# Decay sums one unit earlier, zeroing spread over eight units, the first expert's weights two units later

## The chip, the cores and the metric

The kernel runs on one core of a Trainium2 chip. The metric is device time in microseconds (us) of one execution, as the median of several runs. TensorE is PE in the rows, VectorE is DVE, ScalarE is ACT, GpSimd is POOL, and SyncE, which issues most transfers, is SP.

## The reference

Three layers follow each other. The first is a gated linear attention over 4 sequences of 768 steps with 8 heads of 48; the second sends each of the 3072 rows to one of 8 experts; the third is a gated layer over all rows.

```python
f = 1.0 / (1.0 + np.exp(-f_logit))
for t in range(S):
    state = f[:, :, t, :, None] * state + np.einsum('bhd,bhe->bhde', k[:, :, t], v[:, :, t])
    y[:, :, t] = np.einsum('bhd,bhde->bhe', q[:, :, t], state)
...
e_idx = np.argmax(x @ w_gate, axis=1)
for e in range(E):
    mask = e_idx == e
    h = np.maximum(x[mask] @ w1[e], 0.0)
    out[mask] = gate_w[mask, None] * eom[mask, e, None] * (h @ w2[e])
...
return (1.0 / (1.0 + np.exp(-(x @ w_gate))) * (x @ w_val)) @ w_out
```

## The kernel before, in words

The attention is cut into 24 units of 128 steps, 6 to a sequence. A loop over i = 1 to 23 writes the instructions of several units into each round, and each engine carries its own out in the order written. For a unit u the steps are these. `s_log` and `s_log2` (ACT) make the logarithm of the decays from the tile `ft`. `s_sum` (DVE) sums them along the steps with a scan, 1.2 us long. `s_keys` takes an exponential of the sums on ACT (`gi`) and multiplies the keys by it on DVE (`kT`); `s_queries` takes the other exponential on ACT, in place, and multiplies the queries on POOL (`qT`). `s_end` (ACT) keeps the last decay of each head (`gc_all`). `s_turn` transposes `kT` (PE) and copies it (ACT). `s_score` multiplies keys and queries (PE, `pS`), and `s_mask` masks the result in two halves (DVE, `am`). `s_state` (PE, DVE) carries the state on, `s_y` makes the outputs (PE, `pY`) and copies them (ACT, `xT`), and `s_rows` turns them back into rows together with the router's logits (PE `px`, ACT `x`, DVE `lg`).

Round i holds, in this order: score(i), keys and queries(i+1), the masks of i, y(i-1), state(i), turn(i+1), rows(i-1); log and sum stand in it for unit i+2. So the sum that keys(i+1) reads in round i was written by DVE near the end of round i-1.

Three more kinds of work are woven in. The inputs are asked for ahead on SP's queue (`load`): keys and queries of unit i+4, decays of i+6, values of i+4. A table in HBM, `xs_all`, that later holds each expert's rows, has the rear of each expert's part filled with zeros by 8 transfers from `zrow`, and takes the rows themselves by indirect transfers from POOL (`put_rows`) once `route` has given a group of units their places (on DVE, in short steps that `step_route` takes one or two of per round; the groups are units 0-5, 6-11, 12-16, 17-21, 22-23). And the weights of the first expert come in 10 transfers into 5 staging buffers (`feed.issue`), from which each `feed.step` splits one piece into two parts (ACT `w_hi`, DVE `w_lo`), 14 pieces in all.

After round 23 the expert layer begins with expert 0's first 192 rows (`gather_rows(0)`, `scale`, `to_xt`), whose units call `make_plan` in steps; the plan orders the other experts. `gather_rows(1)`, expert 0's other rows, waits for all rows put.

Of the kernel before, what the change touches and what calls it, by code (L numbers as in the profile page):

```python
# [8 lines left out]
F32 = mybir.dt.float32  # L9
# [3 lines left out]
AF = mybir.ActivationFunctionType  # L13
ALU = mybir.AluOpType
# [6 lines left out]
P = 128  # L21
# [7 lines left out]
def kernel(  # L29
# [17 lines left out]
    nc = tc.nc  # L47
    B, H, S, D = q.shape
    NT, DM = out.shape
    NE = moe_w_gate.shape[1]  # L50
# [3 lines left out]
    HP = H // 2  # L54
# [4 lines left out]
    NB = 4  # L59
    SLOT = NB * P  # L60
# [4 lines left out]
    XW = DM + 2  # L65
# [11 lines left out]
    LEAST = 256  # L77

    PD = P // 2 + D
# [15 lines left out]
    xs_all = drp.tile([NSL, XW], F32, name="xs_all")  # L95
# [391 lines left out]
    st = {}  # L487
# [21 lines left out]
    with ExitStack() as actx:  # L509
# [20 lines left out]
        def load(nm, u):  # L530
            if 0 <= u < NU and (nm, u) not in tin:
                b, c = divmod(u, NCH)
                if nm == "v":
                    t = inp.tile([P, H, D], F32, name="v", bufs=5)
                    nc.sync.dma_start(t.rearrange("p h d -> p (h d)"), v[u * P : (u + 1) * P, :])
                else:
                    t, src = (fts[u % NFT], ft) if nm == "f" else (qks[u % NQK], qkt)
                    for j in (1, 0):
                        nc.sync.dma_start(t[j * (P // 2) : j * (P // 2) + D], src[b, c, j])
                tin[nm, u] = t  # L540

        def s_log(u):

            ln = wk.tile([PD, HP, P], F32, name="ln")
            nc.scalar.activation(out=ln, in_=tin["f", u], func=AF.Exp, scale=-1.0)
            st[u] = dict(ln=ln)

        def s_log2(u):
            ln = st[u]["ln"]
            nc.scalar.activation(out=ln, in_=ln, func=AF.Ln, bias=1.0)  # L550

        def s_sum(u):

            d = st[u]
            d["ls"] = wk.tile([PD, HP, P], F32, name="ls")
            nc.vector.tensor_tensor_scan(  # L556
                out=d["ls"].rearrange("p h t -> p (h t)"), data0=runs01.rearrange("p h t -> p (h t)"),
                data1=d["ln"].rearrange("p h t -> p (h t)"), initial=0.0, op0=ALU.mult, op1=ALU.add,
            )

        def s_keys(u):
# [17 lines left out]
        def s_end(u):  # L579

            nc.scalar.copy(gc_all[:, u, :], st[u]["g"][:, :, P - 1])
# [89 lines left out]
        with tc.manual_schedule():  # L671
            nc.scalar.preload_act_table_set("natural_log_exp_and_others")
            feed.todo = expert_items(0, 0)
            rows_between(nc.vector, fts[0], 30.0)
            nc.gpsimd.memset(oneb, 1.0)
            keep_warm(NWARM)
            nc.vector.memset(rw[D - D % 32 : P // 2, :, PD:], 0.0)
            load("f", 0)
            rows_between(nc.gpsimd, qks[0], 0.0)
            rows_between(nc.vector, fts[1], 30.0)  # L680
            load("f", 1)
            load("qk", 0)
# [12 lines left out]
            load("qk", 2)  # L695
            rows_between(nc.vector, fts[3], 30.0)
            load("f", 3)
            load("v", 1)
            load_router(rw)
            numbers()  # L700
            for u in (0, 1):
                s_log(u)
                s_log2(u)
                load("f", u + 4)
                s_sum(u)
            for u in (0, 1):
                s_keys(u)
                s_queries(u)
                load("v", u + 2)
                load("qk", u + 3)  # L710
            s_turn(0)
            keep_warm(WARM[0])
            s_score(0)
            s_end(0)
            s_log(2)
            s_log2(2)
            s_turn(1)
            load("f", 6)
            load("v", 4)
            for j in range(2):  # L720
                s_mask(0, j)
            s_sum(2)
            s_state(0)
            constants()
            keep_warm(WARM[1])
            groups = [(0, 6), (6, 6), (12, 5), (17, 5), (22, 2)]
            routing = []

            def step_route():
                if routing and next(routing[0], True):  # L730
                    routing.pop(0)

            def on(fn, u, *a):
                if 0 <= u < NU:
                    fn(u, *a)

            for i in range(1, NU):
                if i == NU - 1:
                    gather_rows(0)
                s_score(i)  # L740
                if i == 1:
                    s_log(i + 2)
                    s_log2(i + 2)
                    s_mask(i, 0)
                on(s_keys, i + 1)
                on(s_queries, i + 1)
                load("qk", i + 4)
                on(s_end, i)
                put_rows(2 if i < 19 else 3 if i < 22 else 6)
                if i > 1:  # L750
                    on(s_log, i + 2)
                    s_mask(i, 0)
                load("f", i + 6)
                s_mask(i, 1)
                if i == 1:
                    s_sum(i + 2)
                step_route()
                s_y(i - 1)
                if i > 1:
                    on(s_log2, i + 2)  # L760
                load("v", i + 4)
                s_state(i)
                if i > 1:
                    on(s_sum, i + 2)
                on(s_turn, i + 1)
                if i == 6:
                    feed.issue()
                if i >= 8:
                    feed.step(1)
                if i == LAST:  # L770
                    scale(xg[0], passes[0][2], nc.vector)
                    s_y(i)
                for _ in range(2 if i == LAST else i > 16):
                    step_route()
                s_rows(i - 1)
                for u0, n in groups:
                    if i - 1 == u0 + n - 1:
                        routing.append(route(u0, n))
                if i == 1:
                    nc.gpsimd.memset(zrow, 0.0)  # L780
                if 2 <= i < 6:

                    for e in (2 * i - 4, 2 * i - 3):
                        nc.sync.dma_start(
                            xs_all[e * SLOT + LEAST : (e + 1) * SLOT, :].rearrange("(b p) d -> p b d", p=P),
                            zrow.to_broadcast([P, NB - LEAST // P, XW]),
                        )
            while feed.left():
                feed.step()
            to_xt(0, xg[0], passes[0][2])  # L790
            for todo in routing:
                for _ in todo:
                    pass
            put_rows(6)
            s_rows(LAST)
            for part in range(2):
                put_ids(0, part)
            routing = route(*groups[-1])
            next(routing)

    with ExitStack() as mctx:
# [234 lines left out]
        with tc.manual_schedule():  # L1036
# [24 lines left out]
            for i in range(len(units) + LAG):  # L1061
# [19 lines left out]
                if i < len(units):  # L1081
                    p, f = units[i]
                    if planning:
                        for _ in range(1 if i == 2 else 2):
                            next(planning, None)
                    elif i == 1:
                        for _ in routing:
                            pass
                        put_rows(6)
                        gather_rows(1)  # L1090
                        planning = make_plan()
# [303 lines left out]
```

## Time and profile before

| | |
|---|---|
| median of 3 runs | 847.55 us (847.43 to 851.27) |
| the profiled execution: its time, its span | 854.3 us, 852.5 us |
| PE busy | 823.2 us, 97% |
| DVE, ACT, POOL busy | 450.2, 353.5, 166.9 us |
| moved by all transfers | 87.56 MB |

The span is that of the instructions, the time includes what lies around it. The attention takes about the first 140 us, the expert layer the next 245, the last layer the rest. "Busy" is the sum of instruction times: an engine that is busy 97% over the whole need not be so in each stretch.

### The profile page before, as it was taken

What the parts mean: (1) busy time and instruction counts of PE and PEld (TensorE: products, weight loads), DVE (VectorE), ACT (ScalarE), POOL (GpSimd) and SP (SyncE); (2) the same over time, 40 slices, a digit from 0 to 9 for tenths busy, and PEclk for the clock granted to TensorE, in tenths of its full rate; (3) what the DMA queues carried; (4) which work ended last, traced back from release to release, by engine and by line L of the source; (5) the groups of instructions that cost most, each with busy time, mean ns of one, the idle gap of its engine ahead of it and who ended that gap; (6) DMA issues with size and microseconds to landing.
All of it is one profiled execution on the core that took longest, in us unless ns stands there. A gap on an engine that the chain in (4) does not pass through costs nothing.

```text
span 852.5 us, 13950 instructions
## 1 busy us (share of the span) xinstructions
PE 823.2 (97%) x5289; PEld 727.7 (85%) x5289; DVE 450.2 (53%) x896; ACT 353.5 (41%) x738; POOL 166.9 (20%) x172
## 2 busy tenths in 40 slices
PE   8898989999999999999999999999999999999995
PEld 5776777998899999998888888888888888888884
DVE  6787997568878988997552213222222221232211
ACT  7677874375556665654342212212221221122211
POOL 4225475102323333332000100100010010001001
PEclk9999999999999999999999999999999999999999
DMA  6999762666667767634000200110020010001001
GB/s 158 258 283 266 192 177 82 217 208 196 208 191 224 222 212 218 204 104 139 1 1 1 74 1 1 38 38 0 1 75 1 0 38 2 1 1 38 1 1 40
DMA packets 51645, 87.56 MB, mean 103 GB/s; under 512 B 12874, under 2 KB 32754, under 8 KB 51570
## 3 DMA queue, kind: packets, MB, share of 16 engines
q1 hardware_dynamic: 44946, 62.97, 26.0%
q0 software_dynamic: 6624, 23.62, 8.6%
q8 instruction: 43, 0.70, 0.4%
q14 instruction: 32, 0.26, 0.1%
HBM read 68.35 MB, written 18.22 MB: 102 GB/s over the span
## 4 chain that ended last, share of the span: by engine, by line
issue 51%; PE 32%; DMA 6%; DVE 4%; ACT 3%; POOL 2%; SPq 0%; POOLq 0%; DVEq 0%; ACTq 0%
PE ph L812 5%; PE po L812 5%; PE po L814 5%; PE po L813 5%; PE ph L813 4%; PE ph L814 4%; DMA qk<-in_qkt_dram 4%; POOL out_dram L1022 2%; DMA xs_all<-zrow 1%; DMA ft<-in_ft_dram 1%; PE ptx L430 1%; DVE ls L556 1%; PE pY L653 1%; ACT gi L565 1%; PE px L494 1%
## 5 line engine op out<-in xcount | busy, mean ns | idle before, releaser
L1150 DVE TENSOR_TENSOR hf<-pv,sg 128x512 f32<-128x512 f32 x72 | 49.8, 692 | 266.7 <-PE pv L814 263.1
L1146 ACT ACTIVATE sg<-pg 128x512 f32<-128x512 f32 x72 | 43.1, 598 | 172.8 <-PE pg L814 172.8
L1153 ACT CAST hh<-hf 128x512 fp32r<-128x512 f32 x72 | 44.7, 620 | 161.1 <-DVE hf L1150 152.2
L1022 POOL DMA_INDIRECT out_dram<-ob,ids x24 | 23.6, 983 | 411.4 <-DVE ob L1021 405.9
L813 PE MATMUL po<-w_lo,hh 128*128 128x384 f32 x288 | 96.6, 335 | 0.0
L812 PE MATMUL po<-w_hi,hh 128*128 128x384 f32 x288 | 96.4, 335 | 0.0
L814 PE MATMUL po<-w_hi,hl 128*128 128x384 f32 x288 | 96.3, 334 | 0.0
L814 PE MATMUL pg<-xt_hi,w_lo 128*128 128x512 f32 x216 | 85.5, 396 | 0.0
L813 PE MATMUL pv<-xt_lo,w_hi 128*128 128x512 f32 x216 | 85.5, 396 | 0.0
L812 PE MATMUL pg<-xt_hi,w_hi 128*128 128x512 f32 x216 | 85.5, 396 | 0.0
L813 PE MATMUL pg<-xt_lo,w_hi 128*128 128x512 f32 x216 | 85.1, 394 | 0.0
L812 PE MATMUL pv<-xt_hi,w_hi 128*128 128x512 f32 x216 | 85.1, 394 | 0.0
L814 PE MATMUL pv<-xt_hi,w_lo 128*128 128x512 f32 x216 | 85.1, 394 | 0.0
L244 DVE TENSOR_TENSOR w_lo<-st,w_hi 128x384 fp32r<-128x384 f32 (+1 forms) x112 | 68.9, 647 | 13.9 <-ACT w_hi L243 13.2
L1154 DVE TENSOR_TENSOR hl<-hf,hh 128x512 fp32r<-128x512 f32 x72 | 49.9, 693 | 49.4 <-ACT hh L1153 49.4
L812 PE MATMUL po<-hh,w_hi 128*128 128x192 f32 (+8 forms) x216 | 74.2, 343 | 0.0
L814 PE MATMUL po<-hh,w_lo 128*128 128x192 f32 (+8 forms) x216 | 74.1, 343 | 0.0
L813 PE MATMUL po<-hl,w_hi 128*128 128x192 f32 (+8 forms) x216 | 73.9, 342 | 0.0
L812 PE MATMUL ph<-xt_hi,w_hi 128*128 128x304 f32 (+7 forms) x192 | 67.9, 354 | 0.9 <-DVE hl L1073 0.9
L193 POOL TENSOR_SCALAR cva<-cva 128x512 f32<-128x512 f32 (+1 forms) x30 | 56.3, 1875 | 62.4 <-ACT cva L192 62.1
L1072 ACT ACTIVATE hh<-ph 128x192 fp32r<-128x192 f32 (+8 forms) x72 | 35.6, 494 | 79.1 <-PE ph L814 73.3
L243 ACT CAST w_hi<-st 128x384 fp32r<-128x384 f32 (+1 forms) x112 | 59.3, 558 | 21.9 <-PE po L813 20.0
(173 smaller groups left out, 1658.1 us busy)
## 6 DMA issues: line engine op xcount, KB each, us to landing
st<-in_moe_w_dram SPq DMA_DIRECT2D x48, 256.0 KB
st<-in_moe_w_dram SPq DMA_DIRECT2D x32, 384.0 KB
qk<-in_qkt_dram SPq DMA_DIRECT2D x48, 192.0 KB
ft<-in_ft_dram SPq DMA_DIRECT2D x48, 96.0 KB
v<-in_v_dram SPq DMA_DIRECT2D x24, 192.0 KB
stg<-in_moe_w_gate_dram POOLq DMA_DIRECT2D x9, 512.0 KB
stg<-in_moe_w_val_dram POOLq DMA_DIRECT2D x9, 512.0 KB
stg<-in_moe_w_out_dram POOLq DMA_DIRECT2D x12, 384.0 KB
```

What stands on the lines that cost most here:

```text
L193: nc.gpsimd.tensor_scalar(out=af, in0=af, scalar1=HW_LEAST, scalar2=HW_MOST, op0=ALU.max, op1=ALU.min)
L243: nc.scalar.copy(hi, src)
L244: nc.vector.tensor_tensor(out=lo, in0=src, in1=hi.bitcast(F32), op=ALU.subtract)
L812: nc.tensor.matmul(ps, lhsT=ah, rhs=bh, start=first, stop=False)
L813: nc.tensor.matmul(ps, lhsT=ah, rhs=bl, start=False, stop=False)
L814: nc.tensor.matmul(ps, lhsT=al, rhs=bh, start=False, stop=last)
L1022: put = nc.gpsimd.indirect_dma_start(out=out[:, :], out_offset=bass.IndirectOffsetOnAxis(ap=idx[g][:, i : i + 1], axis=0), in_=ob, in_offs ...
L1072: nc.scalar.activation(out=hh, in_=pS, func=AF.Relu)
L1146: nc.scalar.activation(out=sg, in_=pg, func=AF.Sigmoid)
L1150: nc.vector.tensor_tensor(out=hf, in0=pv, in1=sg, op=ALU.mult)
L1153: nc.scalar.copy(hh, hf)
L1154: nc.vector.tensor_tensor(out=hl, in0=hf, in1=hh.bitcast(F32), op=ALU.subtract)
```

## The change

The logarithm, its sum and the exponential of a unit share one tile `ls` with 4 buffers, and the scan works in place. From round 4 on, log and sum stand in round i for unit i+3; round 4 does two units' logs. The next decays are asked for in `s_log`. `s_end` moves one unit ahead. The zeroing stands in rounds 2 to 9, one expert each. `feed.issue` moves from round 6 to 8 and `feed.step` from 8 on to 10 on. In round 23 the first step of the routing stands ahead of the masks, and the other two behind `s_rows(22)`. In the expert layer each step of the plan is taken one unit later.

```diff
 def s_log(u):
-    ln = wk.tile([PD, HP, P], F32, name="ln")
-    nc.scalar.activation(out=ln, in_=tin["f", u], func=AF.Exp, scale=-1.0)
-    st[u] = dict(ln=ln)
+    ls = wk.tile([PD, HP, P], F32, name="ls", bufs=4)
+    nc.scalar.activation(out=ls, in_=tin["f", u], func=AF.Exp, scale=-1.0)
+    st[u] = dict(ls=ls)
+    load("f", u + NFT)
...
-                on(s_end, i)
+                on(s_end, i + 1)
+                if 1 < i <= LEAD:
+                    s_log(i + 2)
+                    s_log2(i + 2)
                 put_rows(2 if i < 19 else 3 if i < 22 else 6)
-                if i > 1:
-                    on(s_log, i + 2)
-                    s_mask(i, 0)
-                load("f", i + 6)
+                if i >= LEAD:
+                    on(s_log, i + 3)
+                if i == LAST:
+                    step_route()
+                s_mask(i, 0)
                 s_mask(i, 1)
-                if i == 1:
+                if i <= LEAD:
                     s_sum(i + 2)
-                step_route()
+                if i < LAST:
+                    step_route()
                 s_y(i - 1)
-                if i > 1:
-                    on(s_log2, i + 2)
+                if i >= LEAD:
+                    on(s_log2, i + 3)
                 load("v", i + 4)
                 s_state(i)
-                if i > 1:
-                    on(s_sum, i + 2)
+                if i >= LEAD:
+                    on(s_sum, i + 3)
                 on(s_turn, i + 1)
-                if i == 6:
+                if i == 8:
                     feed.issue()
-                if i >= 8:
+                if i >= 10:
                     feed.step(1)
                 if i == LAST:
+                    s_y(i)
                     scale(xg[0], passes[0][2], nc.vector)
-                    s_y(i)
-                for _ in range(2 if i == LAST else i > 16):
+                elif i > 16:
                     step_route()
                 s_rows(i - 1)
+                if i == LAST:
+                    step_route()
+                    step_route()
...
-                if 2 <= i < 6:
-
-                    for e in (2 * i - 4, 2 * i - 3):
-                        nc.sync.dma_start(
-                            xs_all[e * SLOT + LEAST : (e + 1) * SLOT, :].rearrange("(b p) d -> p b d", p=P),
+                if 2 <= i < 2 + NE:
+
+                    nc.sync.dma_start(
+                        xs_all[(i - 2) * SLOT + LEAST : (i - 1) * SLOT, :].rearrange("(b p) d -> p b d", p=P),
...
-                        for _ in range(1 if i == 2 else 2):
+                        for _ in range(min(i - 2, 2)):
                             next(planning, None)
```

The first place is SP's queue at the first weights. Before, this is the end of round 5 and round 6: `qk`, `ft` and `v` are the inputs, `xs_all<-zrow` a zeroing, `st` a load of weights.

```order
L539 DMA qk_114<-in_qkt_dram 48x1024 x2
L539 DMA ft_113<-in_ft_dram 48x512 x2
L535 DMA v<-in_v_dram 128x384
L784 DMA xs_all<-zrow 128x2x386 x2
L539 DMA qk_115<-in_qkt_dram 48x1024 x2
L539 DMA ft_110<-in_ft_dram 48x512 x2
L535 DMA v<-in_v_dram 128x384
L252 DMA st_748<-in_moe_w_dram 128x512
L252 DMA st_750<-in_moe_w_dram 128x512
L252 DMA st_752<-in_moe_w_dram 128x512
L259 DMA st_754<-in_moe_w_dram 128x2x384
L259 DMA st_756<-in_moe_w_dram 128x2x384
```

With the change, this is round 8 and the end of round 9:

```order
L539 DMA qk_114<-in_qkt_dram 48x1024 x2
L539 DMA ft_113<-in_ft_dram 48x512 x2
L535 DMA v<-in_v_dram 128x384
L252 DMA st_914<-in_moe_w_dram 128x512
L252 DMA st_916<-in_moe_w_dram 128x512
L252 DMA st_918<-in_moe_w_dram 128x512
L259 DMA st_920<-in_moe_w_dram 128x2x384
L259 DMA st_922<-in_moe_w_dram 128x2x384
L790 DMA xs_all<-zrow 128x2x386
L539 DMA qk_115<-in_qkt_dram 48x1024 x2
L539 DMA ft_110<-in_ft_dram 48x512 x2
L535 DMA v<-in_v_dram 128x384
```

The five loads of weights stand two rounds later, one zeroing stands behind them, and one more behind the next round's inputs.

The second place is ACT in round 4. Before, one exponential (L545) and one logarithm (L550) stand around the copies of `pY`:

```order
L565 ACTIVATE gi<-ls 112x512
L574 ACTIVATE ls<-ls 112x512
L581 COPY gc_all<-ls 112x4
L545 ACTIVATE ln<-ft_112 112x512
L668 COPY xT<-pY 112x2x128 x2
L550 ACTIVATE ln<-ln 112x512
L500 COPY x<-px 128x2x96
L500 COPY x<-px 128x2x2x48
```

With the change, two more activations stand ahead of those copies:

```order
L564 ACTIVATE gi<-ls 112x512
L573 ACTIVATE ls<-ls 112x512
L580 COPY gc_all<-ls 112x4
L545 ACTIVATE ls<-ft_112 112x512
L551 ACTIVATE ls<-ls 112x512
L545 ACTIVATE ls<-ft_113 112x512
L667 COPY xT<-pY 112x2x128 x2
L551 ACTIVATE ls<-ls 112x512
L500 COPY x<-px 128x2x96
L500 COPY x<-px 128x2x2x48
```

The third place is DVE in round 23. Before, the two masks (`am`) come first, then the first step of the routing (`m` to `oh`), the scaling of the first rows gathered (`xs`), and the ranking, which reads `pr`:

```order
L607 TENSOR_TENSOR am<-pS,tri 128x512 x2
L167 TENSOR_REDUCE m<-lg 128x5
L168 TENSOR_TENSOR t_2248<-lg,m 128x40
L169 TENSOR_TENSOR sc<-lg,m 128x40
L170 TENSOR_TENSOR sc<-sc,e_75 128x40
L171 TENSOR_REDUCE ms_all<-sc 128x5
L172 TENSOR_TENSOR oh<-sc,ms_all 128x40
L441 TENSOR_SCALAR xs<-xs 128x384
L441 TENSOR_SCALAR xs<-xs 64x384
L176 TENSOR_TENSOR ohf<-oh,lg 128x40
L177 TENSOR_REDUCE sel<-ohf 128x5
L347 TENSOR_TENSOR t_2316<-pr,oh 128x40
```

With the change:

```order
L171 TENSOR_REDUCE ms_all<-sc 128x5
L172 TENSOR_TENSOR oh<-sc,ms_all 128x40
L606 TENSOR_TENSOR am<-pS,tri 128x512 x2
L244 TENSOR_TENSOR w_lo<-st_1659,w_hi 128x384
L441 TENSOR_SCALAR xs<-xs 128x384
L441 TENSOR_SCALAR xs<-xs 64x384
L505 TENSOR_REDUCE lg<-px 128x16
L176 TENSOR_TENSOR ohf<-oh,lg 128x40
L177 TENSOR_REDUCE sel<-ohf 128x5
L347 TENSOR_TENSOR t_2301<-pr,oh 128x40
```

The masks stand behind the first step, the last piece of weights (`w_lo`) is in this round, and `lg`, which reads the products `px` of unit 22, stands ahead of the ranking.

## Rows read from the trace of the kernel before

**Rows 1.** Windows, all engines: stretch, busy us, granted clock, DMA share, GB/s.

```profile
40.00:60.00 20.00, 18.77 (x293) 16.13 (x293) 15.75 (x33) 15.51 (x40) 4.15 (x5) 1.00 1.05 299
60.00:80.00 20.00, 17.30 (x228) 14.46 (x228) 15.07 (x35) 14.45 (x37) 10.04 (x12) 0.91 0.99 239
80.00:100.00 20.00, 17.58 (x280) 14.81 (x277) 18.82 (x44) 17.05 (x45) 8.53 (x8) 1.00 0.87 249
160.00:180.00 20.00, 20.00 (x154) 19.77 (x153) 13.26 (x28) 12.93 (x30) 0.00 (x0) 1.00 0.68 218
```

**Rows 2.** Timeline of PE: start, us, line, operation, idle before and its releaser.

```profile
31.91 1.16 PE L600 MATMUL pS<-qT,kT 48*128 48x128 f32 x16
35.21 1.16 PE L494 MATMUL px<-rw,xT 112*128 112x128 f32 x8
...
45.48 1.16 PE L600 MATMUL pS<-qT,kT 48*128 48x128 f32 x16
...
71.18 0.60 PE L588 MATMUL pk<-ident,kT 112*128 112x112 f32 x4 [1.38 <-DVE kT L567]
...
142.54 0.34 PE L812 MATMUL ph<-xt,w_hi 128*128 128x192 f32 x1
```

**Rows 3.** Timeline of DVE, same columns, where it waited.

```profile
52.47 0.69 DVE L567 TENSOR_TENSOR kT<-qk,gi 112x512 f32<-112x512 f32 x1 [0.58 <-ACT gi L565]
...
57.88 0.69 DVE L244 TENSOR_TENSOR w_lo<-st,w_hi 128x512 fp32r<-128x512 f32 x1 [1.19 <-ACT w_hi L243]
...
64.92 0.69 DVE L567 TENSOR_TENSOR kT<-qk,gi 112x512 f32<-112x512 f32 x1 [0.63 <-DMA qk<-in_qkt_dram]
...
72.90 1.27 DVE L556 TENSOR_TENSOR_SCAN ls<-runs,ln 112x512 f32<-112x512 f32 x1 [0.58 <-ACT ln L550]
...
80.25 0.36 DVE L635 TENSOR_TENSOR sn<-pM,gc_all 112x192 f32<-112x192 f32 x1 [3.23 <-PE px L494]
...
106.27 1.23 DVE L556 TENSOR_TENSOR_SCAN ls<-runs,ln 112x512 f32<-112x512 f32 x1 [0.58 <-ACT ln L550]
...
134.88 1.29 DVE L607 TENSOR_TENSOR am<-pS,tri 128x512 f32<-128x512 f32 x2 [0.65 <-PE pS L600]
...
160.56 1.06 DVE L441 TENSOR_SCALAR xs<-xs 128x384 f32<-128x384 f32 x3
```

**Rows 4.** DMA issues by tensor: queue, count, size of one.

```profile
st<-in_moe_w_dram SPq DMA_DIRECT2D x48, 256.0 KB
st<-in_moe_w_dram SPq DMA_DIRECT2D x32, 384.0 KB
qk<-in_qkt_dram SPq DMA_DIRECT2D x48, 192.0 KB
ft<-in_ft_dram SPq DMA_DIRECT2D x48, 96.0 KB
v<-in_v_dram SPq DMA_DIRECT2D x24, 192.0 KB
...
xs_all<-zrow SPq DMA_DIRECT2D x8, 386.0 KB
```

**Rows 5.** Windows, the stretch in which the clock stood at half.

```profile
73.50:76.90 3.40, 3.40 (x36) 2.85 (x32) 3.11 (x6) 2.54 (x7) 2.93 (x4) 0.50 1.07 256
```

**Rows 6.** Timeline of ACT in round 4.

```profile
33.94 0.63 ACT L545 ACTIVATE ln<-ft 112x512 f32<-112x512 f32 x1
34.72 0.65 ACT L668 COPY xT<-pY 112x256 f32<-112x256 f32 x2 [0.15 <-PE pY L662]
```

**Rows 7.** Timeline of POOL: the first put, and the first after round 23.

```profile
72.91 1.16 POOL L385 DMA_INDIRECT xs_all<-x,sidx  x1 [0.18 <-POOL x L383]
...
142.01 1.00 POOL L385 DMA_INDIRECT xs_all<-x,sidx  x1 [0.23 <-POOL xlate L383]
```

**Rows 8.** Timeline of SP's queue: the gathers of the next rows.

```profile
153.82 3.17 SPq L459 DMA_DIRECT2D xs<-xs_all  x3
```

**Rows 9.** Waits from 141 to 172 us: who, for whom, total, times, longest.

```profile
PE pf L904 <- DVE chk L901: 1.6, 1, 1.6
```

More of the change, by code (lines that the diff above doesn't have):

```diff
@@ L542, in s_log @@
         def s_log(u):
-            ln = wk.tile([PD, HP, P], F32, name="ln")
-            nc.scalar.activation(out=ln, in_=tin["f", u], func=AF.Exp, scale=-1.0)
-            st[u] = dict(ln=ln)
+            ls = wk.tile([PD, HP, P], F32, name="ls", bufs=4)
+            nc.scalar.activation(out=ls, in_=tin["f", u], func=AF.Exp, scale=-1.0)
+            st[u] = dict(ls=ls)
+            load("f", u + NFT)
         def s_log2(u):
-            ln = st[u]["ln"]
-            nc.scalar.activation(out=ln, in_=ln, func=AF.Ln, bias=1.0)
+            ls = st[u]["ls"]
+            nc.scalar.activation(out=ls, in_=ls, func=AF.Ln, bias=1.0)
         def s_sum(u):
-            d = st[u]
-            d["ls"] = wk.tile([PD, HP, P], F32, name="ls")
+            ls = st[u]["ls"].rearrange("p h t -> p (h t)")
             nc.vector.tensor_tensor_scan(
-                out=d["ls"].rearrange("p h t -> p (h t)"), data0=runs01.rearrange("p h t -> p (h t)"),
-                data1=d["ln"].rearrange("p h t -> p (h t)"), initial=0.0, op0=ALU.mult, op1=ALU.add,
+                out=ls, data0=runs01.rearrange("p h t -> p (h t)"), data1=ls, initial=0.0, op0=ALU.mult, op1=ALU.add,
             )
@@ L703 @@
                 s_log2(u)
-                load("f", u + 4)
                 s_sum(u)
@@ L714 @@
             s_end(0)
+            s_end(1)
             s_log(2)
@@ L717 @@
             s_turn(1)
-            load("f", 6)
             load("v", 4)
@@ L725 @@
             keep_warm(WARM[1])
+            LEAD = 4
             groups = [(0, 6), (6, 6), (12, 5), (17, 5), (22, 2)]
@@ L747 @@
                 load("qk", i + 4)
-                on(s_end, i)
+                on(s_end, i + 1)
+                if 1 < i <= LEAD:
+                    s_log(i + 2)
+                    s_log2(i + 2)
                 put_rows(2 if i < 19 else 3 if i < 22 else 6)
-                if i > 1:
-                    on(s_log, i + 2)
-                    s_mask(i, 0)
-                load("f", i + 6)
+                if i >= LEAD:
[3 more added lines that the diff above has]
+                s_mask(i, 0)
                 s_mask(i, 1)
-                if i == 1:
+                if i <= LEAD:
                     s_sum(i + 2)
-                step_route()
+                if i < LAST:
+                    step_route()
                 s_y(i - 1)
-                if i > 1:
-                    on(s_log2, i + 2)
+                if i >= LEAD:
+                    on(s_log2, i + 3)
                 load("v", i + 4)
                 s_state(i)
-                if i > 1:
-                    on(s_sum, i + 2)
+                if i >= LEAD:
+                    on(s_sum, i + 3)
                 on(s_turn, i + 1)
-                if i == 6:
+                if i == 8:
                     feed.issue()
-                if i >= 8:
+                if i >= 10:
                     feed.step(1)
                 if i == LAST:
+                    s_y(i)
                     scale(xg[0], passes[0][2], nc.vector)
-                    s_y(i)
-                for _ in range(2 if i == LAST else i > 16):
+                elif i > 16:
                     step_route()
                 s_rows(i - 1)
+                if i == LAST:
+                    step_route()
+                    step_route()
                 for u0, n in groups:
@@ L780 @@
                     nc.gpsimd.memset(zrow, 0.0)
-                if 2 <= i < 6:
-                    for e in (2 * i - 4, 2 * i - 3):
-                        nc.sync.dma_start(
-                            xs_all[e * SLOT + LEAST : (e + 1) * SLOT, :].rearrange("(b p) d -> p b d", p=P),
-                            zrow.to_broadcast([P, NB - LEAST // P, XW]),
-                        )
+                if 2 <= i < 2 + NE:
+                    nc.sync.dma_start(
+                        xs_all[(i - 2) * SLOT + LEAST : (i - 1) * SLOT, :].rearrange("(b p) d -> p b d", p=P),
+                        zrow.to_broadcast([P, NB - LEAST // P, XW]),
+                    )
             while feed.left():
```

## The prediction

> **What bounds it now.** I read the windows first. From 160 us on PE is busy all the time (20.00 of 20) [rows 1], so whatever the change does, it does by moving the moment at which the expert layer gets going; from there on I take the rest as shifted. Ahead of that the windows change character. From 40 to 60 us the transfer engines are full (share 1.05, 299 GB/s) while DVE has 4 us of idle in 20; from 80 to 100 us DVE is busy 18.82 of 20 and the transfers no longer fill their engines (0.87) [rows 1].
>
> Then the timelines, by round. Round 4 begins with the scores at 31.91, round 7 at 45.48 [rows 2]: 13.57 us for three rounds, 4.52 each, with no idle shown on PE in between. So in these rounds PE itself sets the pace, and an earlier sum gives them nothing. In rounds 7 to 12 DVE stands still again and again: 0.58 us for `gi` (which stood for DVE's own scan), 1.19 for a piece of weights that ACT got late, 0.63 for keys and queries still on their way, 0.58 behind ACT's logarithm, and 3.23 for PE [rows 3]. The last one lies over a stretch of 3.4 us in which the granted clock was 0.50 [rows 5], 1.2 GHz in place of 2.4; ahead of it PE had idled 1.38 us for `kT` [rows 2]. After that DVE runs nearly without a wait until round 20: the timeline from 82 to 120 us has one, 0.58 at 106.27 [rows 3]. There DVE's own work is the length, and moving a scan by a round within it changes nothing.
>
> **Part by part.** *Sums three units ahead.* The scan that `gi` stands for is now a round older. That takes away the 0.58 at 52.47. ACT no longer stands for the scan either, so its logarithms come earlier, and the 0.58 at 72.90 and at 106.27 go too: 1.74 us, of which I count 1.7. Bounds: 0.6, if ACT is late for other reasons, to 1.7.
>
> The price is round 4, which does two logs. Two activations more stand ahead of the copies of `pY`; one takes 0.63 us, and only 0.15 us of wait is there to take them [rows 6]. That is 1.1 us at most; neighbours on ACT overlap a little, and I take 0.8 by which `xT` is later. PE's `px`, which began at 35.21 [rows 2] while `xT` was being copied, moves with it. PE is the bound there, so the 0.8 stays. Bounds 0 and 1.1. The second scan in that round lies on DVE beside PE's 4.52 us; were DVE the bound there, it would cost 1.2.
>
> *Zeroing and weights.* A round's inputs are 2 × 192 + 2 × 96 + 192 = 768 KB [rows 4], 0.79 MB. With two zeroings (772 KB) that is 1.58 MB, at 299 GB/s 5.3 us, against a pace of 4.5: rounds 2 to 5 each fall 0.8 us behind. Round 6 with its five loads (3 × 256 + 2 × 384 KB) needs 2.36 MB, 7.9 us, another 3.4 behind. That debt of some 6 us is what comes due as the late piece of weights (1.19) and the late keys (0.63). With the change rounds 2 to 7 need 1.18 MB, 4.0 us, and are not behind. Round 8 needs 2.75 MB, 9.2 us, and round 9 4.0: 13.2 us against two rounds of some 4.9, so 3.4 behind. Keys are asked for three rounds ahead, which covers that. I count the 1.19 and the 0.63 as gone: 1.8 us, bounds 0 and 1.8. The split of weights keeps its two rounds from asking to using.
>
> The Trainium skill, DMA: Bandwidth & Descriptors, Specifications, gives a core some 358 GB/s of HBM. The row shows full engines at 299, so here the row decides. At the page's figure rounds 2 to 5 would need 4.4 us, less than the pace, and the spreading would gain nothing.
>
> Rounds 8 and 9 lose their `w_lo` (0.69 each [rows 3]; I count 0.6, since the next instruction begins before the end): 1.2 us less on DVE where it is the bound. They come back in rounds 22 and 23, which I count with the end.
>
> *Clock.* With fewer waits on DVE the idle of 1.38 us before `pk` should shrink; DVE's lead over PE grows by the 2.4 us of waits ahead of it. Then the drop at 73.5 goes. It costs PE half of 3.4 us, 1.7. Bounds: 0 (it comes back elsewhere) and 3.2 (all of the wait at 80.25). I take 1.7, since the rest of that wait is PE's backlog.
>
> *The end.* In round 23 the first routing step fills DVE's 0.65 us of wait for the scores [rows 3], but delays the masks by some 0.7 us beyond it. The ranking now stands behind the logits of unit 22, so behind `px` (1.16 us on PE [rows 2]) and the last `w_lo`: I put its end about 1.5 us later than now, relative to the round. Behind it wait the casts of the first pass, whose first product is at 142.54 [rows 2], and the puts of units 17 to 21, the first at 142.01 [rows 7]. All puts must land before the next rows are gathered, at 153.82 [rows 8], and these are scaled at 160.56 [rows 3]. On the other side, the plan's first product no longer stands 1.6 us for `chk` [rows 9], which leaves PE free earlier, but the first pass can end no earlier than the gathered rows. Of the 1.5 us I let 0.9 be covered by the time between gather and scaling, and count 0.6 as loss. Bounds: a loss of 1.5, and a gain of 1.5 if the puts turn out to have room and the 1.6 counts in full.
>
> *Without cost:* the in-place scan (same shape), `s_end` a round earlier (the same instruction in the same place), decays asked for in `s_log` (the same four rounds ahead of use).
>
> *A wait that is added.* The first put, at 72.91 [rows 7], must follow the last zeroing, because both write `xs_all`. Before, that one was long over; now it is asked for in round 9 behind the weights. Behind the put stands `qT` of the next unit on POOL, and PE's scores behind that. By the sum above, round 8 begins near 50, and 13.2 us of transfers end near 63; add up to 3 for landing: 66. The put moves to about 72.9 - 3.6 + 0.8 = 70. So 4 us of room, and no cost.
>
> **Sum**, against the profiled execution's 854.3 us: -1.7 (waits for the scan and the logs), -1.8 (late transfers), -1.2 (`w_lo`), -1.7 (clock), +0.8 (round 4), +0.6 (end) = -5.0: 849.3 us. The execution profiled is 6.75 us above the median; I take the difference as the same there: 847.55 - 5.0 = 842.5 us.
>
> **Rivals.**
> *The clock and the end give it back.* PE still idles somewhere for 1.4 us, so the drop stays (+1.7), and the ranking behind the rows costs its full 1.5 (+0.9), and the logs were not late because of the scan (+1.1): 842.5 + 3.7 = 846.2. For it: DVE's rounds with routing stay longer than PE's, so PE must idle. Against: 1.38 us was the longest such idle between 45 and 130 us, and only behind it did the clock fall there.
> *Transfers were not the limit.* Full engines at 299 GB/s need not mean that fewer bytes come sooner. Then 1.8 falls away: 844.3. For it: PE's pace held in rounds 4 to 6 although the engines were full. Against: the pieces and keys of rows 3 were late just behind the debt reckoned above. The page's figure, named above, would make this the likelier case.
> *The end gains.* The `chk` wait and its idle go at the full 1.6, the puts have room: 842.5 - 0.6 - 1.5 = 840.4, with the clock's 3.2 in full 838.9.
> *Slower: the first put stands for the last zeroing.* From a landing at 70 us on, each us is lost on POOL, and with it `qT` and the scores. Within 1 us of 847.55 it ends with a landing at 75, and it is slower by over 0.5% from 79 on, 16 us after the transfers should be through: say 80, 852.5. The SP queue's order speaks for it, the room of 4 us against.
>
> **How the numbers follow.** 0.5% (4.2 us) is about what a measurement of this kernel tells from no change, so faster means under 843.3, slower over 851.8. The forecast has 0.48, within 841 to 844.5, and two thirds of that is under 843.3. The gain at the end has 0.14. Clock and end giving back 0.18, transfers not the limit 0.12, the put waiting 0.08, of which half is slower. Faster: 0.32 + 0.14 + some 0.06 of the others = 0.52; slower 0.04; the rest, 0.44, the same. Range: all bounds on the good side give 842.5 - 0.8 - 1.5 - 2.1 = 838.1; on the bad side 842.5 + 1.1 + 1.8 + 1.7 + 0.3 + 0.9 = 848.3, which I cut at 847.5, leaving the slow case and the worst of the second one out.
>
> **What would show it.** Right: rounds 8 to 12 at 4.4 to 5.5 us each with no DVE wait for `w_hi`, `qk` or `gi`; transfers under full share from 30 to 48 us and full from 50 to 64; no clock of 0.50 near 70; the first expert product some 5 us earlier; no wait of `pf`. Wrong: a drop of the clock in rounds 9 to 20, POOL standing for `zrow` at its first put, no shorter rounds 8 to 12, or a PE idle before the second pass because the gathered rows are late.

## The result, and the profile after

The changed kernel takes 853.46 us (median of 18, 850.58 to 859.34); the kernel before, on the same chip, 848.27 us (median of 18, 846.27 to 852.81). The ratio is 1.0059, 95% interval 1.0042 to 1.0077: slower by 5.2 us, where 842.5 (838.0 to 847.5) was predicted. The profiled execution took 853.0 us, span 850.8, mean granted clock 0.985; the one of before took 854.3 at 0.992. So the two profiles differ by -1.3 us and the medians by +5.2: the profile of before was 6 us above its median, that of after sits on its own.

Scores of a round start (PE's timeline), in us:

| profile | round 7 | round 12 | round 13 | round 23 | last matmul |
|---|---|---|---|---|---|
| before | 45.48 | 73.19 | 79.48 | 133.68 | 842.84 |
| after | 47.02 | 70.79 | 78.90 | 130.67 | 841.02 |
| after - before, from the column before it | +1.54 | -3.94 | +1.82 | -2.43 | +1.19 |

The windows of after, first two of the stretches of [rows 1], then the three stretches ahead of 160 us in which the clock stood at half (the column behind the engines is the granted clock; in [rows 5] such a stretch was 3.4 us long):

```profile
40.00:60.00 20.00, 20.00 (x318) 17.28 (x317) 17.48 (x41) 18.33 (x47) 6.98 (x5) 1.00 0.99 257
60.00:80.00 20.00, 15.46 (x228) 13.29 (x228) 18.42 (x33) 16.69 (x40) 8.62 (x10) 0.95 0.99 285
...
23.30:30.10 6.80, 6.80 (x52) 6.02 (x56) 5.72 (x10) 3.69 (x8) 2.30 (x2) 0.50 1.07 223
77.90:84.70 6.80, 5.80 (x54) 5.49 (x55) 5.03 (x11) 1.70 (x5) 6.14 (x9) 0.50 0.99 309
142.70:149.50 6.80, 6.80 (x37) 6.76 (x35) 3.31 (x19) 0.86 (x5) 5.42 (x8) 0.50 0.41 151
```

From 40 to 60 us PE is now busy all the time, 1.23 us more than in [rows 1]; that is a part of the gain of rounds 7 to 12. But ahead of 160 us the clock stands at half for three times 6.83 us, before for three times 3.41. PE loses up to half of the 10.2 us more: 5.1 us. A second profile of the kernel before, further down, has 13.7 us at half; against that one it is 3.4 us.

PE's timeline of after names what came ahead of these stretches; the first row is in round 2, the second is `px` of round 4, the last is the plan's product:

```profile
23.23 1.01 PE L587 MATMUL pk<-ident,kT 112*128 112x112 f32 x4 [2.56 <-DVE kT L566]
...
36.77 1.21 PE L494 MATMUL px<-rw,xT 112*128 112x128 f32 x8 [0.86 <-ACT xT L667]
...
78.90 2.08 PE L599 MATMUL pS<-qT,kT 48*128 48x128 f32 x16 [3.30 <-POOL qT L575]
...
141.03 0.35 PE L818 MATMUL ph<-xt,w_hi 128*128 128x192 f32 x1 [1.86 <-DVE xt L412]
...
152.63 0.20 PE L910 MATMUL pf<-chk,onec 128*1 128x10 f32 x2
```

In round 13 PE stands 3.30 us for `qT`. POOL's timeline, and the last zeroing on SP's queue, say why:

```profile
67.44 1.31 POOL L575 TENSOR_TENSOR qT<-qk,ls 112x512 f32<-112x512 f32 x1 [3.11 <-ACT ls L573]
68.70 0.77 POOL L383 COPY x<-meta 128x2 int32<-128x2 int32 x2
74.20 1.16 POOL L385 DMA_INDIRECT xs_all<-x,sidx  x1 [4.73 <-DMA qk<-in_qkt_dram]
...
77.57 1.27 POOL L575 TENSOR_TENSOR qT<-qk,ls 112x512 f32<-112x512 f32 x1
```

```profile
65.78 0.40 SPq L790 DMA_DIRECT2D xs_all<-zrow  x1
```

The first put waits 4.73 us, where it waited 0.18 in [rows 7]. The profile names a DMA of keys, but the put's semaphores are those of the last three zeroings; the last one was asked for at 65.78, 8.4 us ahead of the put. By the landing records it was complete at 73.27, and POOL's wait for its semaphore ended at 73.30. Both puts of that round and then `qT` stand behind it. And DVE's timeline shows something that the kernel before had nowhere in its rounds, where `kT` takes 0.69 us [rows 3]:

```profile
67.67 1.63 DVE L566 TENSOR_TENSOR kT<-qk,gi 112x512 f32<-112x512 f32 x1
...
76.91 2.49 DVE L566 TENSOR_TENSOR kT<-qk,gi 112x512 f32<-112x512 f32 x1
...
101.91 1.73 DVE L566 TENSOR_TENSOR kT<-qk,gi 112x512 f32<-112x512 f32 x1
...
118.44 1.62 DVE L566 TENSOR_TENSOR kT<-qk,gi 112x512 f32<-112x512 f32 x1
```

At 67.67 POOL's `qT` of the same unit had begun 0.23 us earlier, and at 101.91 and 118.44 it was ahead too; the `kT` at 76.91 lies beside the second put and the `qT` of the unit before. In the profile of before `qT` starts 0.77 us behind `kT` in most rounds and never ahead of it. These four `kT` are 4.7 us more of DVE.

In round 23 DVE stands for the logits of unit 22 ahead of the ranking:

```profile
137.73 0.23 DVE L505 TENSOR_REDUCE lg<-px 128x16 f32<-128x64 f32 x1 [1.96 <-PE ptx L430]
```

### The profile page after: what moved, and what is told of

It is laid out like the page before. It is cut to its first block, busy times and chain, and to the rows that moved or that the text cites. A ratio compares the mean times of both kernels' runs of the same rounds, so it can differ in the third digit from the quotient of the medians.

```text
span 850.8 us, 13919 instructions
## 1 busy us (share of the span) xinstructions
PE 824.5 (97%) x5289; PEld 730.8 (86%) x5289; DVE 453.2 (53%) x896; ACT 356.9 (42%) x738; POOL 171.5 (20%) x172
## 4 chain that ended last, share of the span: by engine, by line
issue 50%; PE 39%; DVE 3%; ACT 3%; POOL 2%; DMA 1%; SPq 0%; POOLq 0%; DVEq 0%; ACTq 0%
PE ph L818 5%; PE ph L819 5%; PE ph L820 5%; PE po L818 5%; PE po L820 5%; PE po L819 5%; PE pY L652 2%; PE px L494 2%; PE pS L599 2%; POOL out_dram L1028 2%; PE ptx L430 1%; PE pk L587 1%; PE pY L661 1%; DVE kT L566 1%; DMA ft<-in_ft_dram 1%
## 5 line engine op out<-in xcount | busy, mean ns | idle before, releaser
L243 ACT CAST w_hi<-st 128x384 fp32r<-128x384 f32 (+1 forms) x112 | 59.2, 558 | 20.1 <-PE po L819 20.0
```

The source lines that it names most:

```text
L243: nc.scalar.copy(hi, src)
```

## The experiments

In the table "after" is the changed kernel with a part undone or added; "alone" and "weights" are the kernel before with those parts of the change. Each has 6 to 12 executions. Ratios are to the kernel before on the same chip, with 95% intervals, and are not exactly the quotient of the two medians; half clock is the sum of the stretches at 0.50 ahead of 160 us, idle the longest idle of PE from 50 us to the expert layer's first product, both of the one profiled execution.

| kernel | median us | ratio | half clock | idle, ahead of |
|---|---|---|---|---|
| before again | 851.42 | 1.0005 (0.9981 to 1.0030) | 13.7 | 2.28, `pk` round 9 |
| after again | 853.49 | 1.0038 (1.0019 to 1.0056) | 20.5 | 3.30, `pS` round 13 |
| after, zeroing back | 856.29 | 1.0051 (1.0022 to 1.0079) | 27.3 | 2.57, `pk` round 17 |
| after, end back | 855.11 | 1.0037 (1.0014 to 1.0061) | 17.1 | 2.57, `pk` round 17 |
| after, sums back | 857.98 | 1.0106 (1.0058 to 1.0154) | 13.7 | 6.20, `pS` round 13 |
| after, `qT` behind `kT` | 857.05 | 1.0081 (1.0054 to 1.0108) | 17.1 | 5.23, `pS` round 13 |
| after, zeroing back, `qT` behind `kT` | 855.40 | 1.0053 (1.0034 to 1.0072) | 17.1 | 2.87, `pS` round 22 |
| sums alone | 855.36 | 1.0048 (1.0032 to 1.0064) | 17.1 | 4.48, `pk` round 9 |
| end alone | 858.87 | 1.0047 (1.0016 to 1.0078) | 23.9 | 2.34, `pk` round 9 |
| zeroing alone | 859.27 | 1.0076 (1.0046 to 1.0105) | 20.5 | 6.30, `pS` round 13 |
| weights alone | 849.94 | 0.9963 (0.9938 to 0.9988) | 6.8 | 1.26, `pk` round 20 |
| weights, zeroing | 857.40 | 1.0053 (1.0025 to 1.0081) | 20.5 | 6.48, `pS` round 13 |
| weights, zeroing over by round 7 | 847.99 | 0.9977 (0.9957 to 0.9996) | 10.2 | 1.40, `pk` round 20 |
| weights, plan later | 847.32 | 0.9971 (0.9953 to 0.9989) | 6.8 | 1.39, `pk` round 20 |
| weights, sums | 851.59 | 1.0025 (1.0002 to 1.0049) | 13.7 | 2.56, `pk` round 17 |
| weights, whole end | 851.62 | 1.0015 (0.9994 to 1.0036) | 13.7 | 1.87, `ph` |
| weights, sums, `qT` behind `kT` | 852.47 | 1.0019 (0.9998 to 1.0039) | 20.5 | 2.88, `pS` round 22 |
| weights, zeroing by 7, plan later | 847.79 | 0.9975 (0.9957 to 0.9992) | 13.7 | 1.38, `pk` round 20 |

**One part back at a time.** First theory, W: the put's stand and the half clock behind it are the loss. Its rivals: the new end (T), the sums and round 4's second log (S). The kernel before ran again with no edit:

> The kernel before, unchanged, profiled a second time. If a typical execution of it has fewer half-clock stretches ahead of 155 us than the one profiled (three of 3.41 us there, at 25.7, 73.5 and 152.0), then the profile-to-median offset of 6.75 us was those stretches and waits, and cannot be carried over to the changed kernel: a mean granted clock of 0.994 or more and a time near 848 in most executions. If the offset lies elsewhere, the clock stays near 0.992 and the profile near 854.

Its profile came out like the first one, 854.12 us with 2.28 us of idle ahead of `pk` in round 9; its twelve executions went from 848.66 to 858.35 us, with mean clocks from 0.993 down to 0.981, and each lies within 2.3 us of a line of 0.73 us for 0.001 of the clock. So time and clock vary together from execution to execution, and one profile is one draw. Over the kernels of this study the profiled time lay from 3.0 us under to 6.8 us over the median.

The zeroing back:

```diff
-                if 2 <= i < 2 + NE:
-                    nc.sync.dma_start(
-                        xs_all[(i - 2) * SLOT + LEAST : (i - 1) * SLOT, :].rearrange("(b p) d -> p b d", p=P),
...
+                if 2 <= i < 6:
+                    for e in (2 * i - 4, 2 * i - 3):
+                        nc.sync.dma_start(
+                            xs_all[e * SLOT + LEAST : (e + 1) * SLOT, :].rearrange("(b p) d -> p b d", p=P),
...
```

> The changed kernel with the zeroing as before, two experts each in rounds 2 to 5. Theory W (the first put stands on POOL for the last zeroing, which is asked for behind the weights; behind it come the queries of the next unit, the scores of round 13, and a half clock from 77.9 to 84.7): POOL's wait of 4.73 us at the first put goes, PE's 3.30 us for the queries and the stretch at 77.9 with it, some 6.7 us, less up to 1.5 us because rounds 2 to 5 have more bytes again: 846.8 to 848.5. Rival T (the reordered end, whose half clock from 142.7 costs 3.4 us, is what makes it slower): 852 to 854. Rival S (two logs in round 4 and the start): 852 to 854.

The stand went: the first put at 70.46 behind 0.18 us, rounds 13 and 14 at 75.70 and 79.92, 3.8 and 5.3 us ahead of the profile of before. The time did not follow. Behind three `kT` of 1.6 us, at 82.59, 88.06 and 94.01, the next loss came in round 17:

```profile
94.01 1.63 DVE L566 TENSOR_TENSOR kT<-qk,gi 112x512 f32<-112x512 f32 x1
```

```profile
101.62 0.60 PE L587 MATMUL pk<-ident,kT 112*128 112x112 f32 x4 [2.57 <-DVE kT L566]
```

W alone falls. The last round's order back, as in the kernel before:

```diff
-                if i == LAST:
-                    step_route()
                 s_mask(i, 0)
                 s_mask(i, 1)
...
-                if i == LAST:
-                    step_route()
-                    step_route()
...
-                        for _ in range(min(i - 2, 2)):
+                        for _ in range(1 if i == 2 else 2):
```

> The changed kernel with the order of the last round and the plan's place as before. Theory W: unchanged but for the end's own share, 852 to 854.5. Rival T: the idle of 1.86 us ahead of the first product of the expert layer and the half clock from 142.7 on shrink to what the kernel before had (3.41 us at half), 2 to 5 us less: 848.5 to 851.5.

Nothing to be seen in the median, though the stretch from round 23 to the last matmul shortened from 710.3 to 708.4 us. The sums back to two units (the hunks of `s_log`, `s_log2`, `s_sum`, `s_end` and `LEAD` undone):

> The changed kernel with the sums of decays two units ahead as before (no round with two logs, no longer queue of sums); zeroing, weights and end stay changed. Theory W: the put still stands for the last zeroing, 852 to 854.5; since the rounds are a little longer the put comes later and stands less, so it may be 1 us better. Rival S: 849 to 851, with no 0.86 us of wait for xT in round 4 and no 2.56 us for kT in round 3.

Worse, not better, and with no `kT` over 0.7 us from round 1 on: the put now waited 7.68 us and held `qT` until PE had idled 6.20 us. So with the sums ahead the put stands less, they cost elsewhere, and no part by itself explains the loss.

**The meeting of `kT` and `qT`.** Theory P: DVE's `kT` and POOL's `qT`, each with two tensors of SBUF to read, can't run at the same time, and the sums let `qT` go first. A dependence makes `qT` wait:

```diff
-            nc.vector.tensor_tensor(out=kT, in0=tin["qk", u][:, 1], in1=gi, op=ALU.mult)
+            d["made"] = nc.vector.tensor_tensor(out=kT, in0=tin["qk", u][:, 1], in1=gi, op=ALU.mult).ins
...
-            nc.gpsimd.tensor_tensor(out=qT, in0=tin["qk", u][:, 0], in1=g, op=ALU.mult)
+            made = nc.gpsimd.tensor_tensor(out=qT, in0=tin["qk", u][:, 0], in1=g, op=ALU.mult)
+            tc.add_manual_dep(
+                made.ins, d["made"].name,
+                mybir.DependencyInfo(mybir.DependencyClass.Sync, mybir.DependencyReason.DATA), reason="after the keys",
+            )
```

> The changed kernel, with POOL's product for qT made to wait for DVE's product for kT of the same unit. Theory P (with the sums ahead, qT starts before or with kT; both read two tensors of SBUF, and kT then takes 1.6 us in place of 0.69, four times in the profile of the changed kernel, and never in that of before, where qT starts 0.77 us behind kT): no kT over 0.8 us, DVE 3.7 us less in the rounds where it is the bound, fewer idles of PE and so fewer half-clock stretches: ratio to before 1.000 to 1.003, against 1.006 for the changed kernel. Rival W alone (only the first put's stand for the zeroing costs): no gain, 1.005 to 1.007.

> The changed kernel with the zeroing as before (two experts each in rounds 2 to 5) and with qT waiting for kT. Theories P and W together: neither a stretched kT nor a stand of the first put is left; the lead of 5.3 us that the version with the zeroing back had at round 14 stays up to round 23: ratio 0.993 to 0.998. If the reordered end alone makes the changed kernel slower (rival T), 1.002 to 1.005.

> The kernel before with the sums of decays three units ahead and nothing else. Theory P: stretched kT in three to six rounds, 2.8 to 5.6 us more on DVE, against the 1.7 us of waits that go; ratio 1.002 to 1.006. If the sums ahead are worth what was predicted of them by themselves, 0.998 to 0.9995.

> The changed kernel once more, on the same chip as these, with a second profile. Ratio 1.004 to 1.008; a stand of the first put of 3 us or more; three to five kT over 1.5 us; a mean granted clock of 0.983 to 0.987 in most executions, against 0.991 for before.

The sums alone do cost, as P has it, with four `kT` of 1.6 us; but this run also showed weights that came 5.9 us late:

```profile
59.62 0.62 ACT L243 CAST w_hi<-st 128x512 fp32r<-128x512 f32 x1 [5.90 <-DMA st<-in_moe_w_dram]
```

In the first profile of before this wait of ACT is 1.83 us, in the second 3.48. And making `qT` wait took the long `kT` away (but for one of 2.1 us in round 22) without any gain: in round 22 `qT` now stands behind three puts, and PE 2.87 us for it. The changed kernel again gave 1.0038, and the same three stretches of 6.83 us.

**Each part alone.** The edits are those of the diff, one at a time, on the kernel before. Theory I: what costs is a single long idle of PE, with the half clock that follows.

> The kernel before with the new order of the last round and the plan one step later, nothing else. Theory I (what costs is a single idle of PE of 1.8 us or more: the idle itself and some 3.4 us of half clock behind it): one idle of 1.86 us ahead of the first product of the expert layer in place of 1.09 and 1.6 us in two places, a half-clock stretch of 6.83 us behind it in place of 3.41; from the scores of round 23 to the same product of the expert layer 33.1 us in place of 31.8: ratio 1.001 to 1.003. As predicted (0.6 us of loss, up to 1.5 of gain): 0.998 to 1.001.

> The kernel before with expert 0's weights asked for from unit 8 on, nothing else. If the prediction's gain in rounds 8 to 12 (3.0 us: late transfers 1.8, two pieces 1.2) comes from this part: scores of round 12 near 70.5 in place of 73.2, no stand of the first put, no stretched kT: ratio 0.995 to 0.999. If the two pieces that come back in rounds 22 and 23 and the clock take it away: 0.999 to 1.003.

> The kernel before with the zeroing spread over eight rounds, nothing else; the weights are asked for at unit 6. Theory W in its narrow form (the put stands only because the last zeroings are queued behind the weights of round 8): here the last one is asked for some 4 us earlier and lands about 67, before the first put at 70: no stand, ratio 0.998 to 1.002. If the zeroing is late whatever stands before it: a stand of 2 us or more, ratio 1.003 to 1.007.

> The kernel before with the zeroing spread and the weights from unit 8 on; sums and end as before. Theory W: the first put stands 4 to 6 us for the last zeroing, PE idles 4 us or more ahead of the scores of round 13 and the clock falls to half there: ratio 1.003 to 1.008. If the stand only shows together with the sums ahead: 0.996 to 1.000.

These settle the signs. The weights alone are faster: round 12 at 72.27 us although round 7 was at 46.81, so 25.5 us for five rounds in place of 27.7. The three others are slower. With the zeroing alone the put waits too, though no weights of round 8 are ahead of the last zeroing; first SP's queue, then POOL of that run:

```profile
63.71 0.42 SPq L783 DMA_DIRECT2D xs_all<-zrow  x1
```

```profile
66.89 1.28 POOL L576 TENSOR_TENSOR qT<-qk,ls 112x512 f32<-112x512 f32 x1 [4.24 <-ACT gc_all L581]
68.10 0.31 POOL L383 COPY x<-meta 128x2 int32<-128x2 int32 x2
76.27 1.16 POOL L385 DMA_INDIRECT xs_all<-x,sidx  x1 [7.86 <-issue]
```

By the landing records this zeroing was complete at 69.5 us, 1.1 us behind POOL's copy. The put came 6.8 us later, and the profile shows no wait for that time ("issue"). The two other kernels with this zeroing and the sums as before have the like gap, 6.4 us (after, sums back) and 4.6 (weights, zeroing); in the changed kernel it is 0.9. So the zeroing's landing explains the stand in the changed kernel, and only a part of it in these three. What holds POOL there is open. In each of the three gaps the trace has a load of 8 KB of instructions (here at 73.59), and POOL goes on 1.5 to 1.8 us behind its end; in the short gap of the changed kernel there is none. No run shows whether POOL stood for it.

**What is left open, on the weights alone.** The zeroing spread over rounds 2 to 7, so that it ends ahead of the weights; the plan later; the sums; the whole end:

```diff
-                if 2 <= i < 6:
+                if 2 <= i < 8:
-                    for e in (2 * i - 4, 2 * i - 3):
+                    for e in range(max(i - 2, 2 * i - 8), max(i - 1, 2 * i - 6)):
```

> The kernel before with the weights from unit 8 on and the zeroing spread over rounds 2 to 7 (one expert in rounds 2 to 5, two in rounds 6 and 7), so that the last one is asked for ahead of the weights, some 14 us before the first put. Theory W (the loss of the spread zeroing is the first put's stand for a zeroing that lands late, and nothing else): no stand at the first put, ratio 0.994 to 0.999, like the weights alone (0.9963). Rival (the spreading costs by itself, through more bytes later): 1.000 to 1.005.

> The kernel before with the weights from unit 8 on and the plan one step later; the last round as before. If the plan's step is the good part of the new end: no wait of the plan's first product for its counts (1.2 to 1.6 us before), ratio 0.993 to 0.997, so 1 to 2 us under the weights alone. If the time only moves to another place: equal to the weights alone, 0.996 to 0.998.

> The kernel before with the weights from unit 8 on and the sums of decays three units ahead; zeroing and end as before. Theory P (kT and qT at the same time): three to five kT of 1.6 us, single idles of PE near 2.5 us in rounds 13 to 21, ratio 1.000 to 1.006, so 3 us or more over the weights alone. Rival (the loss of the sums by themselves was the late weights, 5.9 us of wait on ACT in that run, which the later asking takes away): 0.994 to 0.998.

> The kernel before with the weights from unit 8 on and the whole new end. Theory I (the single idle of 1.86 us ahead of the expert layer and the half clock behind it): 1.5 to 4 us over the weights alone, ratio 0.998 to 1.002; against the version with only the plan's step this gives the price of the new order in the last round. Rival (the new end costs nothing): 0.995 to 0.997.

The zeroing, the sums and the end came out as the theories have it, the plan's step as the time that only moves. Asked for by round 7, the zeroing costs nothing: the first put at 71.56 behind 0.18 us. The plan's step costs nothing either (0.9971), so the end's price is the order of the last round: 1.0015 on the same chip, 4.3 us more, with this row of PE ahead of the expert layer:

```profile
140.43 0.38 PE L818 MATMUL ph<-xt,w_hi 128*128 128x192 f32 x1 [1.87 <-DVE xt L412]
```

The sums cost without late weights too. Three meetings in a row, DVE's rows and then POOL's of the same units:

```profile
85.94 1.62 DVE L566 TENSOR_TENSOR kT<-qk,gi 112x512 f32<-112x512 f32 x1
...
91.40 1.63 DVE L566 TENSOR_TENSOR kT<-qk,gi 112x512 f32<-112x512 f32 x1
...
97.36 1.63 DVE L566 TENSOR_TENSOR kT<-qk,gi 112x512 f32<-112x512 f32 x1
```

```profile
85.57 1.45 POOL L575 TENSOR_TENSOR qT<-qk,ls 112x512 f32<-112x512 f32 x1 [0.40 <-ACT ls L573]
91.17 1.32 POOL L575 TENSOR_TENSOR qT<-qk,ls 112x512 f32<-112x512 f32 x1 [4.15 <-DMA ft<-in_ft_dram]
96.64 1.80 POOL L575 TENSOR_TENSOR qT<-qk,ls 112x512 f32<-112x512 f32 x1 [4.15 <-ACT ls L573]
```

Last, `qT` behind `kT` in that version, and the good parts together:

> The version with the weights from unit 8 on and the sums ahead (1.0025), with qT made to wait for kT of its unit. Theory P (the sums' loss is the meeting of kT and qT): no kT of 1.6 us in rounds 4 to 20, no idle of PE near 2.5 us at rounds 17 and 18, rounds 14 to 18 in 21.5 us in place of 24.4, ratio 0.996 to 0.999. Rival (the sums lose for another reason, or the wait only moves the loss to the puts behind qT): 1.001 to 1.005.

> What was good, together: weights from unit 8 on, zeroing spread but over by round 7, plan one step later; sums and the order of the last round as before. If the two small gains add: ratio 0.994 to 0.997. If they sit in waits that PE has anyway: 0.996 to 0.998, as each by itself.

With `qT` behind `kT`, rounds 14 to 18 took 20.1 us in place of 24.4 with the sums and 21.3 without them (weights, zeroing by 7). So the meeting is what the sums cost there. But the rival is right about the time: `qT` now stands behind the puts and PE for it, 1.80 us just ahead of round 14 and again here. With round 13 taken in, the three took 26.0, 28.6 and 25.5 us, so nothing is left of the gain, and the ratio stays at 1.0019.

```profile
127.41 1.16 PE L603 MATMUL pS<-qT,kT 48*128 48x128 f32 x16 [2.88 <-POOL qT L575]
```

The good parts together beat both kernels (0.9975), but no more than the weights by themselves: the zeroing and the plan's step add nothing.

## Why the prediction was wrong

**The transfers and the two pieces of weights** (1.8 + 1.2): right in the main. The weights alone take from the round 7 scores to the round 12 scores 25.5 us in place of 27.7, 2.2 us less of the 3.0, and the median falls by 2.8. DVE's waits of 1.19 and 0.63 are gone there, but at two places more it stands 0.58 us for `gi`. The rival "transfers not the limit" falls with that. The spread zeroing alone also brings these rounds to 25.5 us, and both (zeroing over by round 7) to 25.4: two ways to one gain. But the reason given, that rounds 2 to 7 would not be behind, does not hold: from 30 to 48 us the engines were to be under full, and the changed kernel has them at a share of 0.99, moving 267 GB/s. The Trainium skill, DMA: Bandwidth & Descriptors, Specifications, has the figure that was named there, 358 GB/s, by which rounds 2 to 5 would have had room. No run bears that out.

**The sums** (1.7): the gain is there, the same stretch takes 23.8 us in the changed kernel and 25.5 with the weights alone, 1.7 us. The price was missed. "Without cost" named the scan, `s_end` and the decays, and never asked what `qT` does when its decays are ready early: four long `kT`, 4.7 us on an engine that the prediction itself calls the bound of these rounds. **Round 4's** double log was right: `px` waits 0.86 us for `xT`, 0.8 predicted.

**The added wait** is the step that failed first: "So 4 us of room, and no cost." The zeroing was to land at 66 us, the put to come at 70; the zeroing was asked for only at 65.78 and landed at 73.3, and the put came at 74.20. Three terms were off. Full engines were priced at 299 GB/s, though [rows 1] has them as full (0.99) at 239 in the next 20 us. The sum counted 3.93 MB for rounds 8 and 9; from 50 to 73.3 us the changed kernel moved 6.3 MB, at 272 GB/s and a share of 0.99, so transfers asked for earlier were still under way, and later ones went beside them. And "up to 3" us for the landing, which no run shows, were 7.5 from asking to landing. The fourth rival had the mechanism, and its price for a landing at 73.3, 3.3 us, is what PE idled; its point of decision (a landing at 79) was wrong, because it counted the wait and not the half clock behind it, 6.83 us long, up to 3.4 us more. The windows of the changed kernel, of the share that was to be under full and of rounds 8 to 12:

```profile
30.00:48.00 18.00, 17.14 (x268) 14.66 (x264) 13.41 (x23) 15.09 (x37) 3.85 (x3) 1.00 0.99 267
50.00:73.30 23.30, 22.05 (x349) 18.92 (x347) 22.45 (x54) 20.93 (x53) 6.83 (x7) 1.00 0.99 272
```

**The clock** (-1.7) has the wrong sign, up to +5.1 between the two profiles; the executions agree, with a median clock of 0.985 against 0.988 for the kernel before where both ran again on one chip. The step was "Then the drop at 73.5 goes": the prediction counted the waits that vanish and not the idles that the change itself makes, ahead of round 13 and of the expert layer. The stretch at 23 us is no work of the change: the idle ahead of it came with the weights alone too, 2.47 us.

**The end** (+0.6) was mis-sized at "I put its end about 1.5 us later than now". The ranking ends 10.0 us behind the start of round 23, before 7.8, so 2.3 us later: DVE stands 1.96 us for PE ahead of the logits. 0.8 of it is covered, near the 0.9 let, and the first product comes 10.36 us behind that start in place of 8.86, 1.5 us later where 0.6 was counted. From round 23 to the last matmul it takes 710.3 to 715.7 us in the eight profiles with the new order, all of them with a half-clock stretch there; with the old order 707.2 to 708.4 in the five without one, and 709.0 to 712.4 in the seven with one. The two profiles show 1.2 us of loss; that of before has such a stretch itself. `pf` no longer waits its 1.6 us [rows 9], as predicted, but 1.86 us of idle now stand ahead of the first product, where [rows 2] show none.

**The base** was taken wrong as well: "I take the difference as the same there". The offset of 6.75 us belonged to that execution; by the profiles the change gives -1.3 us, by the medians +5.2.

The parts don't add: alone they come to -0.37, +0.76, +0.48 and +0.47%, 1.34% together, and the change costs 0.38 to 0.59%. That with the sums ahead PE idles less behind the put (3.30 us in place of 6.20) is one reason that the runs show; the rest is open.

## What to carry to other kernels

Where an engine's idle is followed by a lower clock, as in the counts below, weigh an edit also by the longest single idle it makes, not only by the sum of waits it removes. Before work is moved earlier, look at who else reads SBUF in that moment, and before a transfer is moved behind others, at the first instruction that must follow it and at everything queued behind that one. A price in GB/s is to be taken from more than one row of full engines. And with run-to-run differences of this size take several executions and their clocks as the base, never one profile's offset.

## What the runs showed of the chip

**Idle and clock.** In the timelines of PE of all 20 profiles, from 9 to 165 us, I counted the idles and the half-clock stretches that began from the idle's start to 3 us behind its end. Of 52 idles of 0.9 to 1.3 us, 4 had one; of 24 of 1.3 to 1.8 us, 11; of 49 longer ones, 39, with 5.2 us at 0.50 (1.2 GHz in place of 2.4) for each of the 49 on the mean. One stretch of 55 began elsewhere. The stretches were 3.41, 6.83, 10.24 and once 13.65 us long. Of the changed kernel the executions at a mean clock of 0.989 took 850.58 and 851.27 us, that at 0.977 took 859.34.

**DVE and POOL.** `kT` takes 0.69 us alone and 1.62 beside a `qT` that began earlier; a `qT` that begins just behind `kT` takes 1.79 in place of 1.28. The Trainium skill, SBUF — State Buffer, section "SBUF: two separate sides", says that a DVE operation with two inputs in SBUF and a GpSimd operation that reads SBUF share a pair of ports, which whoever starts first holds for its whole instruction. The trace agrees: in the version with the weights and the sums the `kT` at 91.40 ends 0.54 us behind the end of the `qT` that began at 91.17. The rule stood ready for the prediction and was not used.
